# Attention in 128-query blocks of four heads, and a rearranged first chunk, in a fused sliding-window attention and MoE kernel on one core

## The chip, the cores and the metric

The kernel runs on one core of one Trainium2 chip. The core has a tensor engine (PE, with its weight loads shown apart as PEld), a vector engine (DVE), a scalar engine (ACT), GpSimd (POOL) and a queue engine (SP). POOL and SP issue the transfers between device memory and the on-chip buffers; sixteen DMA engines carry them out. The metric is the device time of one execution in microseconds (us). Lower is better.

## The reference

Attention over 8 batches, 8 heads, 576 tokens and head size 64, with a causal window of 128 tokens and a linear position bias per head; then, over the 4608 tokens of 512 features, a product with `w_in`, `h * cos(h)`, and a product with `w_out`. All inputs and the output are float32.

```python
B, H, S, D = q.shape                        # 8, 8, 576, 64
scores = 1.0 / np.sqrt(D) * np.matmul(q, k.transpose(0, 1, 3, 2))
rel = pos[:, None] - pos[None, :]
slopes = 2.0 ** (-8.0 * (np.arange(H) + 1) / H)
bias = slopes[:, None, None] * (-np.abs(rel))[None]
mask = (rel >= 0) & (rel < 128)
attn = softmax(np.where(mask, scores + bias[None], -1e9))
x = np.matmul(attn, v).transpose(0, 2, 1, 3).reshape(B * S, H * D)
h = x @ w_in                                # 512 x 2048
out = (h * np.cos(h)) @ w_out               # 2048 x 512
```

## The kernel before

All matrix work is in bf16, with float32 sums. The kernel is written as a list of operations, each with the buffers that it reads and writes, a cost and a priority. `Plan.schedule` plays this list once while the program is built: it gives each engine, at each step, the operation that can start soonest (within a slack, by priority) and so fixes the order of every engine. On the chip each engine runs its instructions in that order and waits on semaphores. Some operations (copies out of the matrix sums) may go to ACT or DVE; the planner picks. The planner's constants (`SWITCH`, the cost of changing between array modes; `TABLE`, of an ACT table load; `WIRE0`, when the first bytes move) decide only orders.

The tokens are cut into nine chunks of 512 (`CH`), which do not line up with the batches of 576.

- Loads. POOL issues q and k of batches 0 and 1 in a row-interleaved form (`qrows`, `krows`, cast to bf16 on the way), the v blocks, `w_in` in five pieces, `w_out` in four. For later batches it loads q and k as they lie (`qnat`, `knat`, one buffer each), and SP transposes them by DMA into `qt`, `kt` (lines 346 and 349). Batches 0 and 1 are transposed on PE against an identity (line 436) and copied out by ACT and DVE. `POOL` also makes the identity and the distance table `dif` (lines 373 to 384), after issuing its first two loads.
- Attention is done in units. A unit is one pair of heads over 256 queries (`G` 0 or 1), and one tail unit per batch takes all heads over the last 64 queries: nine units a batch. For a unit PE makes scores (line 488, two heads side by side in the two halves of the array's rows; the tail's on line 479), ACT takes the exponential (line 518), DVE multiplies by a table `emask` that holds mask and bias as factors (line 534), PE multiplies by v (lines 566 and 569; tail 553 and 555), and DVE divides by the sums (lines 604 and 606). The result goes, transposed, to `xT`: through PE and a copy (line 634, `x_pe`) if its chunk comes next, else by a DMA transpose on SP (`x_dma`). Units go in groups of two.
- MoE1 multiplies `xT` by `w_in` for one chunk in 16 column blocks of four products of 512 columns (line 670). ACT takes the cosine (as a sine with a shift), DVE multiplies into `gT` (two buffers). For chunk 0 this is done in halves of 256 tokens (line 693).
- MoE2 multiplies `gT` by `w_out`: four tiles of 128 tokens a chunk, 16 products of 512 columns each (line 716). ACT or DVE copies the tile to one of four output buffers `ob`, and SP stores it (line 728).

Before the first chunk nine units run, all of batch 0. Then, for chunk c, come MoE1 of c, a quota of units (`QUOTA`, 9, 9, 12, 12, 8, 8, 5) and MoE2 of c; the planner interleaves them. ACT needs one table for exponentials and another for the sine, so it changes tables twice a chunk. `load_v`, `dma_transposes` and `load_nat` for later batches are put in the list as units are done:

```python
while next_t < B and done >= 9 * (next_t - 1):
    dma_transposes(next_t)
    next_t += 1
    if next_t < B:
        load_nat("q", q, next_t)
        load_nat("k", k, next_t)
```

Of the kernel before, what the change touches and what calls it, by code (L numbers as in the profile page):

```python
# [13 lines left out]
NBLK = 5  # L14
# [20 lines left out]
class Plan:  # L35
# [3 lines left out]
    SWITCH = 95  # L39
    TABLE = 1330  # L40
    WIRE0 = 3700
# [46 lines left out]
    def schedule(self):  # L88
        free = {e: 0 for e in ENG}
        wire = {e: self.WIRE0 for e in ENG}  # L90
# [5 lines left out]
        def reach(o, e):  # L96
# [8 lines left out]
            return t  # L105
        for o in self.all:
            if o.npred == 0:
                avail.append(o)
        order = []
        while avail:  # L110
            phase = next((t for t in tables if left[t]), None)
            best = None
            for e in ENG:
                cand = []
                for o in avail:
                    if e not in o.eng or (o.table is not None and o.table != phase):
                        continue
                    st = max(free[e], reach(o, e))
                    if e == "pe" and o.mode != mode:
                        st += self.SWITCH  # L120
                    cand.append((st, o))
                if not cand:
                    continue
                soon = min(st for st, _ in cand)
                slack = 100 if e == "pe" else 40
                st, o = min(((st, o) for st, o in cand if st <= soon + slack),
                            key=lambda c: (c[1].pri, c[1].seq))
# [7 lines left out]
            if len(o.eng) > 1:  # L135
                o.fn, o.occ, o.lat = o.fn[e], o.occ[e], o.lat[e]
                o.eng = (e,)
            o.start = st
            free[e] = st + o.occ
            if o.dma is not None:  # L140
                wire[e] = max(wire[e], st + 2300) + o.lat
                o.end = max(wire[e], st + o.occ + 1400) + 500
# [12 lines left out]
        assert len(order) == len(self.all)  # L155
        self.span = max(o.end for o in order)
        self.order = sorted(order, key=lambda o: o.start)
        rank = {id(o): i for i, o in enumerate(order)}
        self.order.sort(key=lambda o: (o.start, rank[id(o)]))
# [81 lines left out]
def bass_alibi_sliding__then__act_gcu_kernel(  # L241
# [8 lines left out]
    with ExitStack() as ctx:  # L250
# [8 lines left out]
        XR = NTOK  # L259
        xT = sb("xT", [128, NPAIR, XR])  # L260
        gT = [sb(f"gT{i}", [128, NFC, CH]) for i in range(2)]
        qB = {"q": sb("qrows", [128, 2, 1152]), "k": sb("krows", [128, 2, 1152])}
# [3 lines left out]
        EM = sb("emask", [128, H, 512])  # L266
        EMt = sb("emtail", [128, H, 128])
        NP = 4
        P = [sb(f"p{i}", [128, 2, 512]) for i in range(NP)]
        Pt = [sb(f"ptail{i}", [128, 1088]) for i in range(2)]  # L270
        NX = 8
        xnat = [sb(f"xnat{i}", [128, 256]) for i in range(NX)]
        xtl = [sb(f"xtail{i}", [64, 512]) for i in range(2)]
        NCOS = 3
# [4 lines left out]
        ident = sb("ident", [128, 128])  # L279
        halfpi = sb("halfpi", [128, 1], F32)  # L280
# [4 lines left out]
        QUOTA = [9, 9, 12, 12, 8, 8, 5]  # L285
# [3 lines left out]


# [7 lines left out]
        def query_ap(b, x, pr, blk, width):  # L298
# [4 lines left out]
            t = t.rearrange("p (c k t) -> p c k t", c=NBLK, k=NPAIR)  # L303
            if width <= 128:
                return t[lo, blk, pr, 0:width]
            return t[lo, blk:blk + width // 128, pr, :]

        PIECES = {0: [(0, 8, [(0, 4), (4, 8)]), (256, 10, [(0, 5), (5, 10)])],  # L310
                  1: [(0, 18, [(0, 5), (5, 10), (10, 14), (14, 18)])]}

        def piece_keys(which, b, n):
            return [("qB", which, 0), ("qB", which, 1)] if b else [("qB", which, n)]

        def load_qk(which, src, b, n=0):
            t0, R, _ = PIECES[b][n]
            c0 = 64 * (t0 // 32)
            rows = bass.AP(src.tensor, src[b].offset + 64 * t0,
                           [[64 * R, 32], [64 * S, H], [1, 64 * R]])  # L320
            op("pool", [lambda e: e.dma_start(qB[which][:, :, c0:c0 + 64 * R], rows)],
               w=piece_keys(which, b, n), dma=f"ld{which}{n}", occ=800, lat=161 * R)
# [33 lines left out]
        def load_w_in(f0, f1):  # L356

# [3 lines left out]
               w=[("wi", f) for f in range(f0, f1)], dma=f"wi{f0}", occ=800,  # L361
               lat=1300 * (f1 - f0))

        def load_w_out(u):
# [3 lines left out]
               w=[("wo", u)], dma=f"wo{u}", occ=800, lat=2650)  # L368


        def constants():
            sel = ["sel"]
            op("pool", lambda e: e.memset(ident[:, :], 1.0), w=["ident"] + sel)
# [472 lines left out]
```

## Time and profile before

| what | value |
|---|---|
| median of 3 runs | 325.03 us |
| lowest and highest run | 322.65 and 328.85 us |
| span of the profiled execution, first to last instruction | 321.4 us |
| PE busy | 307.3 us |
| ACT, DVE, POOL busy | 203.9, 188.7, 96.6 us |
| read from and written to device memory | 36.70 and 9.44 MB |

The profile is of one execution; its own time is not given beside its span. A row of the timeline gives start, duration, engine, line, operation, output and inputs, and how many instructions; "L716" is line 716 of the kernel above. A matrix product's busy time includes its way through the array, so products that follow closely overlap, and the mean of one (379 ns for 512 columns) is longer than the distance between two. "Idle before" is the time for which an engine stood still, with what ended it.

### The profile page before, as it was taken

Reading aid. Unit: us, or ns where it says so; the run is one execution under the profiler, and the core shown is the slowest. Engines: PE = TensorE matmul, PEld = TensorE weight load, DVE = VectorE, ACT = ScalarE, POOL = GpSimd, SP = SyncE. Lnnn points to the kernel's source line nnn. Section 1 sums busy time; section 2 is a strip of 40 time slices with the busy share of each in tenths; the row PEclk is TensorE's granted clock in tenths of the full one; section 3 lists DMA queues with packets and bytes.
Section 4 is the critical chain, followed back from the end, with each engine's and each line's share of the span. In section 5 each row is a group of like instructions: output and inputs, shape, how many; then the busy total and the mean of one; then the engine's idle time right before and its main releaser. Section 6 shows DMA issues by size and latency. Waiting matters only on the chain.

```text
span 321.4 us, 6210 instructions
## 1 busy us (share of the span) xinstructions
PE 307.3 (96%) x2450; PEld 153.1 (48%) x2450; DVE 188.7 (59%) x414; ACT 203.9 (63%) x296; POOL 96.6 (30%) x124
## 2 busy tenths in 40 slices
PE   2789999999999999999999999999999999999995
PEld 2568745434544554455444544544444444444442
DVE  3689759674777677759684856564653550344000
ACT  5797865885688696866686676665674562453211
POOL 7997141355347572744507200000000000000000
PEclk9999999999999999999999999999999999999999
DMA  6999999999999999999999982131013001201121
GB/s 89 170 206 210 205 160 192 143 168 144 164 140 160 163 197 146 193 154 153 153 131 122 171 135 45 63 81 45 2 65 76 34 0 55 77 0 67 65 92 72
DMA packets 145004, 37.82 MB, mean 118 GB/s; under 512 B 134224, under 2 KB 139856, under 8 KB 144976
## 3 DMA queue, kind: packets, MB, share of 16 engines
q0 software_dynamic: 100144, 18.36, 74.7%
q1 hardware_dynamic: 44832, 19.08, 29.9%
q8 instruction: 19, 0.31, 0.4%
q14 instruction: 9, 0.07, 0.1%
HBM read 36.70 MB, written 9.44 MB: 144 GB/s over the span
## 4 chain that ended last, share of the span: by engine, by line
PE 82%; DMA 9%; POOL 4%; SPq 2%; issue 1%; ACT 1%; DVE 0%; POOLq 0%; ACTq 0%
PE ps L716 38%; PE ps L670 31%; DMA qrows<-in_q_dram 5%; PE ps L488 4%; DMA xT<-xnat 2%; PE ps L693 2%; DMA kt<-knat 2%; SPq L346 2%; PE ps L566 2%; PE ps L569 1%; POOL vp L327 1%; PE ps L634 1%; PE ps L436 1%; POOL w_inb L358 1%; PE ps L479 1%
## 5 line engine op out<-in xcount | busy, mean ns | idle before, releaser
L716 PE MATMUL ps<-w_outb,gT 128*128 128x512 bf16 x576 | 138.9, 379 | 0.0
L670 PE MATMUL ps<-xT,w_inb 128*128 128x512 bf16 x512 | 116.8, 379 | 0.8 <-DVE xnat L606 0.7
L679 DVE TENSOR_TENSOR gT<-ps,cos 128x512 bf16<-128x512 f32 x128 | 81.2, 685 | 51.0 <-PE ps L716 41.0
L675 ACT ACTIVATE cos<-ps,halfpi 128x512 f32<-128x512 f32 x128 | 81.3, 688 | 37.6 <-PE ps L716 19.1
L716 PEld LDWEIGHTS ps<-w_outb,gT 128*128 128x128 bf16 x576 | 53.6, 98 | 58.6 <-issue 1.9
L670 PEld LDWEIGHTS ps<-xT,w_inb 128*128 128x128 bf16 x512 | 47.2, 98 | 61.5 <-DVE gT L679 6.4
L518 ACT ACTIVATE p<-ps 128x768 bf16<-128x768 f32 (+1 forms) x64 | 55.8, 919 | 23.8 <-PE ps L488 18.7
L534 DVE TENSOR_TENSOR p<-p,emask 128x768 bf16<-128x768 bf16 (+1 forms) x64 | 38.3, 616 | 7.4 <-ACT p L518 6.8
L327 POOL DMA_DIRECT2D vp<-in_v_dram x40 | 33.8, 869 | 27.2 <-PE ps L569 16.2
L722 ACT ACTIVATE ob<-ps 128x512 f32<-128x512 f32 x24 | 14.4, 601 | 36.9 <-PE ps L716 36.8
L337 POOL DMA_DIRECT2D qnat<-in_q_dram x30 | 25.2, 875 | 28.4 <-DMA qt<-qnat 28.4
L337 POOL DMA_DIRECT2D knat<-in_k_dram x30 | 25.3, 875 | 25.7 <-DMA kt<-knat 23.7
L606 DVE TENSOR_TENSOR xnat<-ps,rec 128x256 bf16<-128x256 f32 x64 | 24.4, 420 | 1.1 <-DMA xT<-xnat 0.8
L488 PE MATMUL ps<-qt,kt 64*128 64x128 bf16 (+1 forms) x320 | 19.4, 247 | 1.4 <-DMA kt<-knat 1.2
L566 PEld LDWEIGHTS ps<-vp,p 128*128 128x128 bf16 x256 | 15.8, 98 | 7.1 <-issue 3.2
L566 PE MATMUL ps<-vp,p 128*128 128x65 bf16 x256 | 18.5, 195 | 0.0
L604 DVE RECIPROCAL rec<-ps 128x4 f32<-128x4 f32 x64 | 8.2, 167 | 17.4 <-PE ps L569 17.0
L488 PEld LDWEIGHTS ps<-qt,kt 64*128 64x128 bf16 x320 | 11.4, 96 | 13.2 <-issue 4.9
L569 PE MATMUL ps<-vp,p 128*128 128x65 bf16 x192 | 17.2, 194 | 0.0
L693 PE MATMUL ps<-xT,w_inb 128*128 128x256 bf16 x128 | 16.2, 273 | 0.8 <-ACT xT L643 0.5
L724 DVE COPY ob<-ps 128x512 f32<-128x512 f32 x12 | 8.3, 688 | 13.4 <-PE ps L716 13.4
L569 PEld LDWEIGHTS ps<-vp,p 128*128 128x128 bf16 x192 | 13.5, 98 | 0.5
(51 smaller groups left out, 167.6 us busy)
## 6 DMA issues: line engine op xcount, KB each, us to landing
out_dram<-ob SPq DMA_DIRECT2D x36, 256.0 KB, 2.1
vp<-in_v_dram POOLq DMA_DIRECT2D x32, 128.0 KB, 8.1
qnat<-in_q_dram POOLq DMA_DIRECT2D x24, 128.0 KB, 6.2
knat<-in_k_dram POOLq DMA_DIRECT2D x24, 128.0 KB, 4.9
w_outb<-in_moe_w_out_dram POOLq DMA_DIRECT2D x4, 512.0 KB, 21.8
w_inb<-in_moe_w_in_dram POOLq DMA_DIRECT2D x3, 512.0 KB, 10.6
qrows<-in_q_dram POOLq DMA_DIRECT2D x1, 576.0 KB, 14.9
krows<-in_k_dram POOLq DMA_DIRECT2D x1, 576.0 KB, 16.9
```

What stands on the lines that cost most here:

```text
L327: op("pool", [lambda e, t=t, rows=rows: e.dma_start(vp[b % 2][0:rows, t, :, 0:64], v[b, :, 128 * t:128 * t + rows, :].rearrange("h p d -> ...
L337: fns.append(lambda e, t=t, rows=rows: e.dma_start(nat[which][0:rows, t, :, :], src[b, :, 128 * t:128 * t + rows, :].rearrange("h p d -> p ...
L488: ins = e.matmul(ps[:, banks[x], c0:c1], keys_ap(b, x, pr, kc), query_ap(b, x, pr, qb, 128 * nb), start=True, stop=True)
L518: op("act", lambda e: e.activation(P[i][:, :, lo:512], src_[:, :, lo:512], ACTF.Exp, scale=0.125), w=held + [("P", i)], occ=920 if G else ...
L534: op("dve", lambda e: e.tensor_tensor(P[i][:, :, lo:512], P[i][:, :, lo:512], EM[:, h0:h1 + 1, lo:512], ALU.mult), r=[("P", i), ("EM", h0) ...
L566: ins = e.matmul(o, P[i][:, x, d0:d0 + 128], V[:, kc, h, 0:65], start=True, stop=not two)
L569: ins = e.matmul(o, P[i][:, x, p0:p0 + 128], V[:, kc - 1, h, 0:65], start=False, stop=True)
L606: op("dve", lambda e: e.tensor_tensor(o, U[:, :, :, 0:64], rv[:, :, :, None].broadcast_to([128, 2, 2, 64]), ALU.mult), r=[("rec", n % 2)], ...
L670: op("pe", lambda e, kc=kc: e.matmul(ps[:, bank, :], w_in[:, kc, 128 * fc:128 * fc + 128], xT[:, kc, r0:r0 + CH], start=(kc == 0), stop=(k ...
L675: op("act", lambda e: e.activation(cosb[ci][:, :], ps[:, bank, :], ACTF.Sin, bias=halfpi[:, 0:1]), r=["halfpi"], w=[("B", bank), ("cos", c ...
L679: op("dve", lambda e: e.tensor_tensor(gT[gi][:, fc, :], ps[:, bank, :], cosb[ci][:, :], ALU.mult), r=[("cos", ci)], w=[("B", bank), ("g", ...
L716: op("pe", lambda e, t=t, fc=fc, bank=bank: e.matmul(ps[:, bank, :], gT[gi][:, fc, 128 * t:128 * t + 128], w_out[:, fc, :], start=(fc == 0 ...
```

## The change

- A unit is now one block of 128 queries by four heads (`(b, qb, hh)`, `qb` 1 to 3). The first block of a batch, whose window holds no earlier keys, is one unit of all eight heads, and so is the 64-query tail: eight units a batch. Scores are always 128 columns wide (64 in the tail). All eight-head units use both sum banks `UB`; a batch's first block is normalised into a new buffer `xfirst` and transposed in four.
- Seven units, the 512 tokens of chunk 0, come before the first chunk; quotas are 8, 8, 8, 8, 8, 8, 9, and the later loads follow `8 * (next - 1)`.
- MoE1 of chunk 0 goes by blocks of 128 tokens and four column blocks.
- q and k of batch 0 come in three pieces instead of two. The first (128 tokens) is loaded by SP in float32 and cast by ACT or DVE (`qcast`, `kcast`). POOL makes its constants before its loads, and the loads are interleaved in a new order.
- For three of the first units the bias is added by PE, as a product of the identity with a table `bias`, before the scores are summed on top; these units skip the multiplication on DVE. `emask` is made from `bias` by two exponentials.
- PE starts with 19 products of a block of zeros.
- The very last output tile is made and stored as 384 and 128 columns.
- The planner has start times for each engine, doubled PE costs before 8 us, other costs for loads, and another rule of choice for PE.

In the built program PE has 448 + 128 score products instead of 320 + 128, 576 products with v as before, 48 + 32 + 28 transposes of x instead of 66, 128 transposes in the row-interleaved form and 8 whole ones instead of 144, and 256 products for MoE1 of chunk 0 instead of 128. SP transposes 25 results by DMA instead of 39.

```diff
-    SWITCH = 95
+    SWITCH = 110
     TABLE = 1330
-    WIRE0 = 3700
+    START = {"pe": 1300, "act": 750, "dve": 1050, "pool": 550, "sp": 750}
+    COLD = 8000
+    FILL = 107
...
+        def pick_pe(cand):
+            soon = min(st for st, _ in cand)
+            first = [(st, o) for st, o in cand if o.pri < 5 and st <= soon + 160]
+            if first:
+                return min(first, key=lambda c: (c[1].pri, c[1].seq))
+            near = [(st, o) for st, o in cand if st <= soon]
+            return min(near, key=lambda c: (c[1].pri, c[1].seq))
...
-        QUOTA = [9, 9, 12, 12, 8, 8, 5]
+        QUOTA = [8, 8, 8, 8, 8, 8, 9]
+        BIASED = [(0, 0, 0), (0, 1, 0), (0, 1, 1)]
...
-        PIECES = {0: [(0, 8, [(0, 4), (4, 8)]), (256, 10, [(0, 5), (5, 10)])],
+        PIECES = {0: [(0, 4, [(0, 4)]), (128, 4, [(0, 4)]), (256, 10, [(0, 5), (5, 10)])],
...
+            if b == 0 and n == 0:
+                op("sp", [lambda e: e.dma_start(qF[which][:, :, :], rows)],
+                   w=[("qF", which)], dma=f"ld{which}f", occ=400, lat=600)
+                i = qF[which][:, :, :].rearrange("p y (j d) -> p y j d", j=4)
+                o = qC[which][:, :, :, :].rearrange("p j y d -> p y j d")
+                op(("act", "dve"),
+                   {"act": lambda e: e.activation(o, i, ACTF.Copy),
+                    "dve": lambda e: e.tensor_copy(o, i)},
+                   r=[("qF", which)], w=piece_keys(which, b, n), occ={"act": 460, "dve": 330},
...
         def masks():
+            flat = dif[:, :, :].rearrange("p a b -> p (a b)")
             for h in range(H):
...
+                    "dve": lambda e, o=o, s=s: e.tensor_scalar(o, flat, s, None, ALU.mult)},
+                   r=["dif"], w=[("BT", h)], occ={"act": 310, "dve": 250},
+                   lat={"act": 410, "dve": 330}, pri=3)
+            for x in range(2):
+                op("act", lambda e, x=x: e.activation(
+                    EM[:, x, :, :], BT[:, x, :, :], ACTF.Exp, scale=0.125),
...
         def units(b):
-            return [(b, pr, G) for G in range(2) for pr in range(NPAIR)] + [(b, "t", None)]
+            return [(b, 0, 0)] + [(b, qb, hh) for qb in range(1, 4) for hh in range(2)] + [
+                (b, 4, 0)]
...
+                    if qb == 0:
+                        jobs = [(128 * pr, 128, pr, 0) for pr in range(NPAIR)]
+                    elif qb == 4:
+                        jobs = [(128 * pr + 64 * i, 64, pr, 3 + i) for pr in range(NPAIR)
+                                for i in range(2)]
+                    else:
+                        jobs = [(256 * i + 128 * j, 128, 2 * hh + i, qb - 1 + j)
+                                for i in range(2) for j in range(2)]
...
+                        op("pe", lambda e, rhs=rhs, bank=bank: e.matmul(
+                            ps[:, bank, :], ident[:, :], rhs, start=True, stop=False),
...
+        def moe1_block(t, f4, bank):
+            for i in range(4):
+                    for kc in range(NPAIR):
+                        ins = e.matmul(
+                            ps[:, bank, 128 * i:128 * i + 128],
+                            w_in[:, kc, 128 * fc:128 * fc + 128], xT[:, kc, t0:t0 + 128],
...
+                for n, (j0, j1) in enumerate([(0, 384), (384, 512)] if last else [(0, 512)]):
...
         load_qk("q", q, 0, 1)
         load_qk("k", k, 0, 1)
-        load_v(0)
+        load_v(0, [0])
+        load_qk("q", q, 0, 2)
+        load_qk("k", k, 0, 2)
+        load_v(0, [1])
+        load_w_in(0, 1)
+        load_v(0, [2])
+        load_w_in(1, 2)
+        load_v(0, [3])
+        load_w_in(2, 4)
+        load_w_in(4, 6)
...
         load_qk("q", q, 1)
+        load_w_in(6, 8)
         load_qk("k", k, 1)
+        load_v(0, [4])
...
-        attention(every[0:9], -1)
-        done = 9
+        done = 7
+        attention(every[0:done], -1)
...
+                order = [(0, 0), (1, 0), (2, 0), (0, 1), (1, 1), (2, 1), (3, 0), (3, 1)] + [
+                    (t, f4) for f4 in (2, 3) for t in range(4)]
+                for i, (t, f4) in enumerate(order):
+                    moe1_block(t, f4, seq[i % 6])
...
-        R.schedule()
+        R.schedule(filler=lambda e: e.matmul(ps[:, UB[1], 0:128], zeros[:, :], zeros[:, :],
+                                             start=True, stop=True), fill=(1300, 7500))
```

496 lines of the change are left out of this document (259 added, 237 removed).

## The prediction

> **What bounds the kernel now.** I read the page first, then busy time by stage, then the chain of waits in the stretches where the stages show idle time, then the loads.
>
> ```profile
> span 321.4 us, 6210 instructions
> ...
> PE 307.3 (96%) x2450; PEld 153.1 (48%) x2450; DVE 188.7 (59%) x414; ACT 203.9 (63%) x296; POOL 96.6 (30%) x124
> ```
>
> ```profile
> 0.00:20.80 20.80, 12.07 (x182) 8.21 (x183) 12.96 (x38) 14.43 (x24) 19.09 (x32) 1.00 1.26 147
> 20.80:38.90 18.10, 17.95 (x241) 14.96 (x238) 15.20 (x31) 15.01 (x24) 11.27 (x14) 1.00 1.20 207
> 38.90:72.90 34.00, 32.82 (x269) 15.65 (x268) 24.45 (x54) 24.41 (x35) 11.68 (x14) 1.00 1.95 167
> 72.90:289.20 216.30, 215.53 (x1636) 101.34 (x1637) 132.40 (x286) 142.91 (x203) 54.55 (x65) 1.00 1.00 106
> ```
>
> The second fence is busy time by stage: the stretch, its length, then busy time of PE, weight loads, DVE, ACT, POOL, then granted clock, DMA share, GB/s. From 20.8 us on PE hardly rests; before that 8.7 us are idle, and a good part of the 12.1 "busy" is slow or small. So nothing but the front, a few waits and PE's own work can move the time. The front ends where MoE2 of chunk 0 starts, at 38.9. I split the span there: 38.9 of front, 282.5 behind it.
>
> What sets the 38.9? The chain of waits from 14 to 40 us, and the issues and landings of the loads (line, KB each, us to landing; the last row is the w_in tile's minimum, median, maximum):
>
> ```profile
> 14.24 14.86 DMA qrows<-in_q_dram
> ...
> 32.07 0.68 PE ps L436 x20
> ...
> 34.17 0.62 PE ps L436 x16
> ...
> 36.42 0.57 PE ps L436 x16
> 36.99 2.07 PE ps L693 x18
> 39.06 1.08 PE ps L716 x5
> ```
>
> ```profile
> 1.32 0.83 POOL L321 DMA_DIRECT2D qrows<-in_q_dram  x1 [0.81 <-POOLq L831]
> 2.15 0.72 POOL L321 DMA_DIRECT2D krows<-in_k_dram  x1
> 2.86 0.22 POOL L373 MEMSET ident<- 128x128 bf16 x1
> 4.45 0.29 POOL L384 TENSOR_SCALAR_AFFINE_SELECT dif<-dif 128x128 f32<-128x128 f32 x1
> 4.89 0.75 POOL L321 DMA_DIRECT2D qrows<-in_q_dram  x1 [0.15 <-issue]
> 5.64 0.71 POOL L321 DMA_DIRECT2D krows<-in_k_dram  x1
> 10.57 3.75 POOL L358 DMA_DIRECT2D w_inb<-in_moe_w_in_dram  x5
> 14.94 0.71 POOL L321 DMA_DIRECT2D krows<-in_k_dram  x1
> ```
>
> ```profile
> krows<-in_k_dram POOLq DMA_DIRECT2D x1, 576.0 KB, 16.9
> qrows<-in_q_dram POOLq DMA_DIRECT2D x1, 320.0 KB, 4.4
> krows<-in_k_dram POOLq DMA_DIRECT2D x1, 320.0 KB, 6.0
> krows<-in_k_dram POOLq DMA_DIRECT2D x1, 256.0 KB, 4.8
> ```
>
> ```profile
> DMA to landing us min/median/max: 6.2/8.8/12.4
> ```
>
> POOL issues its loads long before they land: they stand in one queue and land in order. Batch 1's k was issued at 14.94 and landed at 14.94 + 16.9 = 31.8; its transposes run at 32.07, and what hangs behind them fills PE until 38.9, 7.1 us later. The rate: w_in's first piece lands at 10.57 + 6.2 = 16.8, the last (issued about 13.5) at 25.9, so 1792 KB in 9.1 us, 197 KB/us. So the front is a stream of loads up to batch 1's k, plus 7.1 us.
>
> **The front after the change.** Four things move that landing.
> - POOL makes its constants before its first load. They take 2.86 to 4.74, 1.9 us; the first load goes from 1.3 to about 3.0: +1.7 (bounds 1.4 and 1.9).
> - The same constants no longer cut the stream. Batch 0's first k landed at 2.15 + 4.8 = 6.9, the second q only at 4.89 + 4.4 = 9.3 and the second k at 5.64 + 6.0 = 11.6; 320 KB should take 1.6 each by the rate, and took 2.4 and 2.3: -1.5.
> - The first 128 tokens of q and k (128 KB each as bf16) come over SP's queue in float32: -256/197 = -1.3.
> - The fifth block of v (64 KB) goes behind batch 1's k: -0.3.
>
> SP's two float32 loads (issued under 1.5 us) use the DMA engines while the POOL stream has not begun, which hides them; without that cover they hold twice the bytes, at most 512/197 = 2.6 us. Sum -1.4: k lands at 30.4 (29.5 to 32).
>
> Behind that landing stand, in the built order, the same 20 + 16 + 16 transposes of 64 columns (0.68 + 0.57 + 0.57), and 60 MoE1 products of 128 columns where 44 of 256 stood. Before, 18 took 2.07 with one switch of array mode, so 0.109 each; half is 0.055. The trace's nearest whole 128-wide products are x transposes, two in 0.16. I take 0.058 (0.055 to 0.08): 3.5, with switches 5.6. Front: 30.4 + 5.6 = **36.0**, 2.9 less.
>
> Is PE ready for that? The stream's first 256 KB should land at 3.0 + 4.8 = 7.8, and the first w_in piece 1152 KB later, at 13.7 instead of 16.8. From there PE has 256 x 0.058 = 14.8 of MoE1, 2.5 of batch 1's four transposes with 0.6 of switches, and about 4 of attention (four units at 0.3 of scores, 0.3 of p-v, 0.2 of x, and switches): 35.6. ACT was busy 15.0 of 18.1 us in that stage and has two exponentials fewer. So the stream is last, by 0.4 us; the earlier start of attention, the bias on PE (six 512-wide products while PE waits), the zero products and the earlier casts all end in a wait for the stream, and I price them at nothing. If the stream were earlier, PE would be next, so 0.4 us is all they can add.
>
> **Behind the front.** Rows from the chain of waits, the kt tile's transposes (ns minimum/median/maximum) and the waits table (longest in the last column):
>
> ```profile
> 58.52 7.08 SPq L346
> ...
> 65.64 7.20 DMA kt<-knat
> ...
> 72.88 0.50 PE ps L488 x8
> 73.39 3.13 PE ps L716 x14
> 76.52 0.44 PE ps L488 x8
> 76.95 0.32 PE ps L716
> ...
> 78.50 0.16 PE ps L634 x2
> 78.66 0.22 PE ps L716
> 78.99 0.55 PE ps L488 x12
> ```
>
> ```profile
> L346 SPq DMA_TRANSPOSE kt<-knat x6: 2672/3455/7078, 58.5 to 183.8; - x6
> ```
>
> ```profile
> PE ps L488 <- DMA kt<-knat: 1.2, 1, 1.2
> PE ps L670 <- DVE xnat L606: 0.7, 1, 0.7
> ```
>
> - Score groups: columns and p-v products are the same in sum, but the built order has 29 groups behind the front instead of 33. A lone MoE2 product after a group takes 0.32 instead of 0.22, and the way in costs as much: 4 x 0.22 = -0.9. 16 products of 128 keep the 0.55 of 12.
> - Seven units, not nine, precede the front; their sums leave batch 0's tail behind it: 16 p-v products and a quarter of a group, +0.7.
> - x through PE: behind the front 25 pairs become 18 pairs, 7 transposes of four (a batch's first block) and 7 narrow ones of four: 25 x 0.16 = 4.0 becomes 2.9 + 2.2 + 1.3 = 6.4: +2.4. SP loses 14 of 39 x transposes.
> - Wait for batch 2's kt, 1.2. PE reaches those scores with 73 MoE2 products done where it had 57, so at 36.0 + 137 x 0.216 + 6.4 = 72.0 (before, 72.9 - 1.2 - 38.9 less 121 x 0.216 left 6.7 for one unit more). kt: its transposes follow the same stream, 1.4 earlier, so 71.5 or before; v of batch 3 is no longer queued ahead of them. -1.2 (0 to -1.2).
> - Wait for x at 156, 0.7: x by DMA is now needed a whole chunk later. -0.7.
> - Uniform quotas of 8, six P buffers, the planner's new constants: no price of their own, 0 ± 1; PE is 99.6% busy in that stage.
>
> ```profile
> 318.20 0.60 ACT ob L722
> ...
> out_dram<-ob SPq DMA_DIRECT2D x36, 256.0 KB, 2.1
> ```
>
> - The last tile is split 384/128: the last copy shrinks from 0.60 to about 0.27, the last product ends 0.16 sooner, the store of 64 KB may save 0.2; the 384 part is stored while PE still works. -0.7.
>
> Sum -0.9 + 0.7 + 2.4 - 1.2 - 0.7 - 0.7 = -0.4: 282.1 behind the front. Span 36.0 + 282.1 = **318.1**, 3.3 under this profile's. The profile's 321.4 lies 1.25 under the fastest time, 322.65, and 3.6 under the median of 325.03; of launch and end nothing is shown, so I carry the difference to the median: **321.7 us**.
>
> **A rule against it.** POOL's issues are 0.69 to 0.95 long wherever DVE stands:
>
> ```profile
> L327 POOL DMA_DIRECT2D vp<-in_v_dram x20: 687/877/945, 6.4 to 59.2; - x20
> ```
>
> The Trainium skill, SBUF — State Buffer, section "Who interferes with whom", says that a VectorE operation in a two-port mode, float32 copies among them, locks GpSimd out of writing descriptors. The change puts two such casts and four bias products on DVE just when POOL writes its first descriptors. By that rule the stream would slip by their length, by the planner's own costs 4 x 0.25 + 2 x 0.33 = 1.7 us, an estimate; the row's spread of 0.26 bounds it far lower. As a mechanism of this kernel it is rival B.
>
> **Rivals.**
> - A: the runs that make the median lie up to 6 us over the fastest (322.65 to 328.85), and what can lengthen a run here is a late transfer: kt at 72.9 is waited for already, and up to 12 units a chunk were demanded. At 8 units a batch is due every 33 us, so after could lose that too, 3.6: 325.0 - 3.3 - 3.6 = 318.1. Against: the one wait shown is 1.2, no more. 0.36.
> - B: the stream is not earlier, since constants first, float32 loads and DVE's port work take back the 1.4 and more: front 38.5, 325 or a little under. 0.10.
> - C, slower: SP's queue. Batch 3's transposes stand ahead of MoE2 stores, and each pair held SP's queue from 58.5 to landing for 14 us. If qt must also wait for the loads of q, which now wait for the transposes before them, stores stop, four output buffers fill, and PE stands. It decides once a chunk's 28 us of transposes plus stores and x exceed 33; one chunk in each batch at 2 us gives 12: 333. Against: the median issue of kt is half of this first one's, and 14 x transposes leave SP. 0.09.
>
> My forecast has 0.45. Two per cent, about what a measurement of this kernel can tell from no change, is 6.5 us. Faster by more: two thirds of A and a fifth of the forecast, 0.33; slower: C, 0.09; within: 0.58. Range: the forecast's own terms give 319 to 325; with A and B 315 to 326.5.
>
> **What would show it.** MoE2 of chunk 0 starts at 36 (38 or later: B), batch 1's k lands near 30.4, the scores of batch 2 begin near 72 with no wait on kt, no x wait over 0.3 later, end behind the last product 2.6 instead of 3.2. PE standing behind full output banks between 70 and 250 us would be C. If the front is 36 and the span not under 320, my price for x through PE is wrong.

## The result and the profile after

The kernel after took 321.6 us (median of 12 runs, 320.88 to 322.64) beside 322.86 for the kernel before on the same chip: ratio 0.9956, 95% interval 0.9937 to 0.9976. Run once more later, beside other versions, it took 320.73 against 324.16: 0.9902, 0.9867 to 0.9936. So there is a gain, between 0.2 and 1.3%; the two ratios differ mostly by the kernel before, whose median was 322.86 in one set and 324.16 in the other. The time agrees with the 321.7 that was forecast, but its parts don't: the front did not shrink, what lies behind it shrank by more than forecast, and the step from span to time was half of the one carried over. That the sum agrees is luck. One version below, x by DMA, was profiled in an execution of 334.28, over 1.5% longer than its fastest of 328.65, so its figures by stage are of a slow execution.

The page of the kernel after, then its busy time by stage (columns as in the prediction: stretch, length, PE, weight loads, DVE, ACT, POOL, granted clock, DMA share, GB/s):

```profile
span 320.0 us, 6788 instructions
...
PE 307.2 (96%) x2741; PEld 163.0 (51%) x2781; DVE 196.9 (62%) x424; ACT 203.4 (64%) x277; POOL 96.6 (30%) x124
```

```profile
0.00:8.00 8.00, 5.88 (x55) 3.64 (x55) 5.50 (x23) 4.95 (x8) 6.71 (x16) 1.00 0.78 120
8.00:16.00 8.00, 3.72 (x55) 2.73 (x58) 2.21 (x5) 3.31 (x6) 5.84 (x8) 0.79 1.49 167
16.00:24.00 8.00, 7.53 (x148) 5.87 (x145) 6.42 (x18) 7.35 (x9) 6.92 (x10) 1.00 1.36 204
24.00:39.50 15.50, 15.29 (x297) 14.37 (x296) 13.15 (x23) 12.48 (x20) 10.98 (x14) 1.00 1.24 206
39.50:320.00 280.50, 274.74 (x2197) 136.37 (x2234) 169.60 (x356) 175.26 (x238) 66.19 (x79) 1.00 1.02 107
```

PE is nearly full from 16 us on; the hole is in the second row, where it is busy for 3.7 us of 8. The chain of waits of the front (start, length, what) shows whose hole it is, and the PE timeline what was waited for:

```profile
5.37 7.33 DMA qrows<-in_q_dram
...
17.60 0.38 PE ps L756 x4
...
39.50 1.67 PE ps L784 x7
```

```profile
12.74 1.28 PE L483 MATMUL ps<-ident,qrows 128*64 128x128 bf16 x20 [3.12 <-DMA qrows<-in_q_dram]
14.35 0.63 PE L555 MATMUL ps<-bias,ident 128*128 128x512 bf16 x1 [0.33 <-issue]
14.78 0.63 PE L675 MATMUL ps<-ident,xfirst 128*128 128x128 bf16 x4
15.35 0.56 PE L541 MATMUL ps<-qt,kt 64*128 64x128 bf16 x8
15.83 0.75 PE L483 MATMUL ps<-ident,krows 128*64 128x128 bf16 x20
...
33.66 0.75 PE L483 MATMUL ps<-ident,krows 128*64 128x128 bf16 x20
```

The third piece of q (320 KB; "the large piece" below) was issued at 5.37 and landed 7.33 us later; PE stood for 3.12 us in front of its transposes, while bias products, x transposes and scores that needed nothing from it stood behind them in PE's fixed order. MoE1 began at 17.60, MoE2 of chunk 0, "MoE2(0)" below, at 39.50. So the front is 39.5 (before 38.9), and 280.5 lie behind it (before 282.5). The load that the prediction took for the last of the stream, batch 1's k, was issued at 17.13 and landed at 32.73 (31.83 in the kernel before, 30.4 in the forecast). PE came to its transposes at 33.66, the last row, 0.9 later: in this profile PE was last, and not the stream.

Behind the front the waits table has nothing left over 0.2 us, and the last copy starts 2.4 us ahead of the end, where it was 3.2:

```profile
PE ps L784 <- issue: 1.6, 10, 0.2
```

```profile
316.71 0.49 ACT L791 ACTIVATE ob<-ps 128x384 f32<-128x384 f32 x1 [2.00 <-PE ps L784]
...
317.60 0.28 ACT L791 ACTIVATE ob<-ps 128x128 f32<-128x128 f32 x1 [0.40 <-PE ps L784]
```

### The profile page after: what moved, and what is told of

It is laid out like the page before. It is cut to its first block, busy times and chain, and to the rows that moved or that the text cites. A ratio compares the mean times of both kernels' runs of the same rounds, so it can differ in the third digit from the quotient of the medians.

```text
span 320.0 us, 6788 instructions
## 1 busy us (share of the span) xinstructions
PE 307.2 (96%) x2741; PEld 163.0 (51%) x2781; DVE 196.9 (62%) x424; ACT 203.4 (64%) x277; POOL 96.6 (30%) x124
## 4 chain that ended last, share of the span: by engine, by line
PE 90%; ACT 3%; DMA 2%; issue 2%; POOL 1%; DVE 1%; ACTq 0%; POOLq 0%
PE ps L784 39%; PE ps L731 32%; PE ps L541 5%; PE ps L756 4%; DMA qrows<-in_q_dram 2%; PE ps L615 2%; PE ps L617 2%; ACT p L568 2%; PE ps L483 1%; PE ps L675 1%; PE ps L603 1%; PE ps L694 1%; DVE gT L740 1%; ACT cos L736 1%; PE ps L607 1%
## 5 line engine op out<-in xcount | busy, mean ns | idle before, releaser
L784 PE MATMUL ps<-w_outb,gT 128*128 128x512 bf16 (+2 forms) x566 | 133.2, 373 | 2.4 <-issue 1.6
L731 PE MATMUL ps<-xT,w_inb 128*128 128x512 bf16 x499 | 113.2, 379 | 0.7
L568 ACT ACTIVATE p<-ps 128x1024 bf16<-128x1024 f32 x64 | 62.0, 1021 | 30.4 <-PE ps L541 30.3
L731 PEld LDWEIGHTS ps<-xT,w_inb 128*128 128x128 bf16 x512 | 48.9, 98 | 59.1 <-DVE gT L740 3.5
L587 DVE TENSOR_TENSOR p<-p,emask 128x1024 bf16<-128x1024 bf16 x61 | 41.0, 684 | 6.4 <-ACT p L568 6.2
L791 ACT ACTIVATE ob<-ps 128x512 f32<-128x512 f32 (+2 forms) x25 | 14.5, 581 | 36.8 <-PE ps L784 36.8
L654 DVE TENSOR_TENSOR xnat<-ps,rec 128x256 bf16<-128x256 f32 x48 | 18.3, 419 | 0.1
L756 PE MATMUL ps<-xT,w_inb 128*128 128x128 bf16 x256 | 16.8, 219 | 0.2 <-DVE rec L652 0.2
L615 PEld LDWEIGHTS ps<-vp,p 128*128 128x128 bf16 x192 | 12.7, 97 | 7.2 <-issue 6.4
L615 PE MATMUL ps<-vp,p 128*128 128x65 bf16 x192 | 15.2, 193 | 0.3
L617 PE MATMUL ps<-vp,p 128*128 128x65 bf16 x192 | 15.2, 193 | 0.0
L756 PEld LDWEIGHTS ps<-xT,w_inb 128*128 128x128 bf16 x256 | 14.5, 98 | 0.9 <-issue 0.3
L617 PEld LDWEIGHTS ps<-vp,p 128*128 128x128 bf16 x192 | 12.5, 97 | 0.0
## 6 DMA issues: line engine op xcount, KB each, us to landing
w_outb<-in_moe_w_out_dram POOLq DMA_DIRECT2D x4, 512.0 KB, 19.8
```

What stands on the lines that cost most here:

```text
L568: op("act", lambda e: e.activation(P[i][:, 0:1024], ps[:, banks[0]:banks[0] + 2, :].rearrange("p a b -> p (a b)"), ACTF.Exp, scale=0.125), ...
L587: op("dve", lambda e: e.tensor_tensor(p, p, m, ALU.mult), r=[("P", i), ("EM", 0), ("EM", 1)], w=[("P", i)], occ=600, lat=690, pri=1)
L615: e.matmul(o, P[i][:, c0:c0 + 128], V[:, qb - 1, h, 0:65], start=True, stop=False)
L617: ins = e.matmul(o, P[i][:, c0 + 128:c0 + 256], V[:, qb, h, 0:65], start=False, stop=True)
L731: op("pe", lambda e, kc=kc: e.matmul(ps[:, bank, :], w_in[:, kc, 128 * fc:128 * fc + 128], xT[:, kc, r0:r0 + CH], start=(kc == 0), stop=(k ...
L756: ins = e.matmul(ps[:, bank, 128 * i:128 * i + 128], w_in[:, kc, 128 * fc:128 * fc + 128], xT[:, kc, t0:t0 + 128], start=(kc == 0), stop=( ...
```

## The experiments

The question was what holds the front at 39.5: the stream of loads (theory S), PE's own added work and its order (P), or DVE holding back POOL's descriptors (D, the prediction's rival B). All versions start from the kernel after. The table collects them; medians and ratios are against the kernel before in the same set, the other columns come from each version's one profile. "k" is batch 1's k: when it landed, and when PE came to its transposes.

| version | median us | ratio (95% interval) | large piece of q landed | k landed, reached | MoE2(0) starts | behind it |
|---|---|---|---|---|---|---|
| after | 321.6 | 0.9956 (0.9937 to 0.9976) | 12.70 | 32.73, 33.66 | 39.50 | 280.5 |
| after, again | 320.73 | 0.9902 (0.9867 to 0.9936) | 11.53 | 32.78, 32.82 | 38.43 | 280.7 |
| last tile whole | 321.9 | 0.9939 (0.9913 to 0.9965) | 11.35 | 31.39, 32.51 | 38.13 | 281.5 |
| v early | 320.75 | 0.9913 (0.9885 to 0.9941) | 12.67 | 33.06, 34.26 | 39.88 | 280.3 |
| no zero products | 321.21 | 0.9924 (0.9898 to 0.9950) | 11.89 | 31.93, 33.47 | 39.31 | 280.5 |
| POOL loads before constants | 320.71 | 0.9909 (0.9882 to 0.9935) | 10.92 | 32.82, 32.87 | 38.58 | 280.5 |
| first q, k by POOL in bf16 | 324.66 | 1.0022 (0.9993 to 1.0052) | 13.08 | 33.12, 34.23 | 40.30 | 280.9 |
| wait filled | 321.85 | 0.9948 (0.9924 to 0.9971) | 11.39 | 32.06, 33.44 | 39.06 | 281.1 |
| x by DMA | 332.39 | 1.0234 (1.018 to 1.0288) | 11.41 | 33.01, 33.06 | 38.55 | 294.0 |
| MoE1 in halves | 320.67 | 0.9914 (0.988 to 0.9948) | 12.23 | 32.22, 33.20 | 37.68 | 281.9 |
| no bias on PE | 323.0 | 0.9977 (0.9947 to 1.0006) | 12.69 | 32.69, 35.35 | 41.20 | 281.1 |
| loads first, v later | 320.41 | 0.9882 (0.985 to 0.9914) | 9.55 | 31.71, 31.75 | 37.59 | 281.1 |
| the same, in halves | 319.78 | 0.9864 (0.9832 to 0.9896) | 9.73 | 31.47, 31.51 | 37.48 | 280.6 |

The k column shows a second limit of the front, which was not among the theories. In five profiles PE comes to the transposes of batch 1's k 0.04 or 0.05 us behind its landing, and in three of them the row shows a wait, as here:

```profile
32.87 0.75 PE L483 MATMUL ps<-ident,krows 128*64 128x128 bf16 x20 [1.03 <-DMA krows<-in_k_dram]
```

```profile
31.75 0.75 PE L483 MATMUL ps<-ident,krows 128*64 128x128 bf16 x20 [0.40 <-DMA krows<-in_k_dram]
```

The first row is of the version with POOL's loads before its constants, the second of the one with v later; with x by DMA the wait is 0.39. From PE's start on these transposes MoE2(0) follows 5.5 to 6.1 us later in all versions but halves (4.5). So the stream up to batch 1's k plus some 5.6, the prediction's own limit, holds the front where PE would come to these transposes earlier.

**The same kernel again.**

> The kernel after, once more, beside the three others of this set. In four profiles with its early order on PE the large piece of q landed at 11.35 to 12.70, by how far one of the 16 DMA engines lagged, and MoE2(0) started 26.8 to 27.4 us behind that landing. Theory S: so again here, front = landing + 27.0 within 0.5, and 280.5 behind it. Theory P (PE alone sets the front): MoE2(0) at 39.5 wherever the piece lands.

From PE's timeline of this second profile:

```profile
11.57 1.28 PE L483 MATMUL ps<-ident,qrows 128*64 128x128 bf16 x20 [0.74 <-DMA qrows<-in_q_dram]
...
38.43 1.89 PE L784 MATMUL ps<-w_outb,gT 128*128 128x512 bf16 x8
```

The piece landed 1.17 sooner, and MoE2(0) started 1.07 sooner. Over the four profiles that share PE's order (after twice, last tile whole, v early) the front is the landing plus 26.8 to 27.2. S holds here; P, which had 39.5 whatever lands, falls. The first w_in piece moves along with it (front 23.0 to 23.3 behind its landing), but what PE's first MoE1 product waits for last is DVE (0.16 to 0.47 in these four), with w_in there 1.1 us or more before.

**Without the zero products.**

```diff
-    start=True, stop=True), fill=(1300, 7500))
+    start=True, stop=True), fill=(0, 0))
```

> The kernel after without its 19 zero products; nothing else moves. Theory S (stream): the front, up to MoE2 of chunk 0, is set by when the second large piece of q (320 KB) and the first w_in piece land (12.7 and 16.5 us), with about 22 us of PE work behind w_in. The zero products end in that wait, so MoE2(0) still starts at 39.5 and the time moves by less than 0.3 us. Theory P (PE): PE's own early work sets the front, so its first products run at a lower clock without the zeros, the granted clock falls in the slices after 4 us, and the front grows by 0.5 to 1 us.

```profile
11.93 1.28 PE L483 MATMUL ps<-ident,qrows 128*64 128x128 bf16 x20 [1.32 <-DMA qrows<-in_q_dram]
...
39.31 1.67 PE L784 MATMUL ps<-w_outb,gT 128*128 128x512 bf16 x7
```

PE's early products were slower (see the last section), and the front is landing plus 27.4, 0.2 to 0.6 more than with the zeros; the runs (320.19 to 323.52) can't be told from the kernel after's. About 0.6 us at most, then.

**POOL's first two loads ahead of its constants.**

```diff
-        constants()
         load_qk("q", q, 0, 1)
         load_qk("k", k, 0, 1)
+        constants()
```

> POOL issues its two loads of q and k (tokens 128 to 255) before it makes its constants, as the kernel before did with its first loads. If the stream's volume from POOL's first issue on sets the landing of the second large piece of q (12.7), that piece lands 1 to 1.6 us sooner and MoE2(0) starts at 38 to 38.5. If that landing follows from its own issue (5.37, unmoved here, since POOL does the same work before it), it stays near 12.7 and the front at 39.5; the first landings alone (6.1 and 7.1) come 1.6 sooner.

```profile
10.96 0.75 PE L483 MATMUL ps<-ident,qrows 128*64 128x128 bf16 x20 [1.17 <-DMA qrows<-in_q_dram]
...
38.58 1.67 PE L784 MATMUL ps<-w_outb,gT 128*128 128x512 bf16 x7
```

The piece was issued 0.6 later than in the kernel after (5.98) and landed 1.8 sooner (10.92; 0.6 sooner than in the second profile): neither reading as written. MoE2(0) gained less than the piece, since PE then stood 1.03 for batch 1's k; without that wait the front would be some 37.6, an estimate from these rows. What differs is in the landings of the piece's 16 parts, one for each DMA engine. From its issue to the median of the 16 it takes 4.24 to 4.77 us in thirteen of the fourteen kernels (5.03 in one), the kernel before included; from the median to the last it takes:

```
before 0.17, POOL loads first 0.56, loads first and v later 0.41, the same in halves 0.41
after 2.75, again 1.39, last tile whole 1.24, v early 2.56, no zeros 1.73, no bias 2.45,
wait filled 1.12, halves 2.05, x by DMA 1.00, first q and k by POOL 1.15
```

In the first row nothing or one load is issued directly ahead of the piece (the constants come between); in the others three loads follow each other without a pause, and the last part comes 1.0 to 2.75 us behind the median, in most profiles with one to three others 0.7 or more behind it too. So the landing of this piece is its own issue plus about 4.5, plus a laggard. The smaller loads ahead of it took less, 2.9 to 4.3 to the median of theirs.

**The first 128 tokens over POOL's queue in bf16.** SP's float32 loads and DVE's casts are gone.

```diff
-            if b == 0 and n == 0:
+            if False:
...
-            whole = b == 0 and n == 0
+            whole = False
```

> The first 128 tokens of q and k come over POOL's queue in bf16, as in the kernel before, instead of over SP's in float32 with casts on DVE. POOL gets two more issues, about 1.6 us, ahead of all else. Theory S: the large piece of q and all behind it land 1.3 to 1.6 us later and MoE2(0) starts near 41. Theory D (the float32 loads or the two DVE casts hold the stream back, as a rule on DVE and POOL sharing a port would have it): without them the piece lands no later than 12.7 for all that, POOL's issues of 0.70 to 0.92 become shorter, and the front stays or shrinks.

```profile
13.12 0.75 PE L483 MATMUL ps<-ident,qrows 128*64 128x128 bf16 x20 [0.30 <-DMA qrows<-in_q_dram]
...
40.30 1.67 PE L784 MATMUL ps<-w_outb,gT 128*128 128x512 bf16 x7
```

The piece was issued 1.9 later (7.28), its median engine had it 2.0 later, and the ratio rose to 1.0022 from 0.9902 to 0.9956, 2 to 4 us. Without the casts the piece took the usual 4.65 from its issue to the median, so D is not what made it late. The two casts and the issues beside them, first in the kernel after, then in the version with MoE1 in halves:

```profile
4.19 0.53 DVE L360 CAST qcast<-qfirst 128x512 bf16<-128x512 f32 x1 [0.45 <-DMA qfirst<-in_q_dram]
4.82 0.81 DVE L360 CAST kcast<-kfirst 128x512 bf16<-128x512 f32 x1
3.78 0.72 POOL L364 DMA_DIRECT2D krows<-in_k_dram  x1
4.49 0.89 POOL L370 DMA_DIRECT2D vp<-in_v_dram  x1
5.37 0.70 POOL L364 DMA_DIRECT2D qrows<-in_q_dram  x1
```

```profile
4.00 0.43 DVE L360 CAST qcast<-qfirst 128x512 bf16<-128x512 f32 x1 [0.26 <-DMA qfirst<-in_q_dram]
4.68 0.43 DVE L360 CAST kcast<-kfirst 128x512 bf16<-128x512 f32 x1 [0.25 <-DMA kfirst<-in_k_dram]
3.78 0.79 POOL L364 DMA_DIRECT2D krows<-in_k_dram  x1
4.57 1.02 POOL L370 DMA_DIRECT2D vp<-in_v_dram  x1
5.58 0.70 POOL L364 DMA_DIRECT2D qrows<-in_q_dram  x1
```

Of a cast and the issue beside it, one is stretched. In the nine profiles with this order of POOL's issues, k's issue takes 0.72 where the first cast takes 0.53 to 0.62, and 0.78 to 0.83 where that cast takes 0.43; v's takes 0.89 where the second cast takes 0.60 to 0.87, and 1.02 to 1.06 where that one takes 0.43. The rule of the Trainium skill, SBUF — State Buffer, section "Who interferes with whom", by which these casts can shut POOL out of writing descriptors, agrees with these rows. But it is small here: the large piece is issued at 5.37 to 5.67 in these nine, so 0.3 us at most, where rival B needed 1.4 and more.

**The wait filled.** The planner is told that the large piece lands 2.5 us later.

```diff
-               ..., lat=161 * rr)
+               ..., lat=161 * rr + (2500 if b == 0 and n == 2 and which == "q" else 0))
```

> The planner is told that the large piece of q lands 2.5 us later than it believed, so PE's order has two bias products, eight scores and the four transposes of the first block ahead of that piece's transposes instead of behind them. Theory S with a fixed order: 1.5 to 1.8 us of PE work moves into the wait of 3.1 us (9.6 to 12.7), and as PE has no gap behind it, MoE2(0) starts 1 to 1.8 us sooner, at 37.7 to 38.5. Theory W (w_in's landing at 16.5 alone decides): MoE1 still starts near 17 and the front shrinks by 0.5 at most. The order behind the front changes too, so that part may move by 0.5 either way.

```profile
11.95 1.27 PE L484 MATMUL ps<-ident,qrows 128*64 128x128 bf16 x20
14.28 1.28 PE L484 MATMUL ps<-ident,krows 128*64 128x128 bf16 x20 [1.06 <-ACT qt L498]
...
39.06 1.89 PE L785 MATMUL ps<-w_outb,gT 128*128 128x512 bf16 x8
```

A miss. The work did move into the wait, but PE then waited 1.06 for a copy, ran its products at the slow pace until 18 us, and the front is landing plus 27.7. Shifting this work bought nothing. That the chain from q over scores, exponentials, p-v and x to MoE1 is last fits this, but this version doesn't separate it from the slow pace.

**MoE1 of chunk 0 in halves of 256 tokens.**

```diff
+        def moe1_half(hf, f2, bank):
...
-                order = [(0, 0), (1, 0), (2, 0), (0, 1), ...]
-                    moe1_block(t, f4, seq[i % 6])
+                order = [(0, f2) for f2 in range(8)] + [(1, f2) for f2 in range(8)]
+                    moe1_half(hf, f2, seq[i % 6])
```

> MoE1 of chunk 0 goes in halves of 256 tokens and two column blocks, as in the kernel before, instead of blocks of 128 tokens and four; all else is of the kernel after, with the order that the planner makes of it. Theory S (the front is the landing of the early loads and then PE's work): 128 products of 256 cost 14.0 where 256 of 128 cost 14.8, but the first can start only when all of x for 256 tokens is there, some 1 us later, so MoE2(0) starts between 38.5 and 40 and the part behind stays at 280.5. Rival (the blocks of 128 are what keeps PE fed before 20 us): the idle time of PE between 16 and 24 us grows from 0.5 to over 2 and the front exceeds 41.

```profile
37.68 1.46 PE L813 MATMUL ps<-w_outb,gT 128*128 128x512 bf16 x6
```

Neither reading: MoE2(0) starts sooner than both have it and 281.9 lie behind it, since the planner leaves some of batch 1's transposes for later; the sum, 319.6 with the piece at 12.23, is what the kernel after has at such a landing. Blocks of 128 buy nothing, halves cost nothing.

**No bias on PE.**

```diff
-        BIASED = [(0, 0, 0), (0, 1, 0), (0, 1, 1)]
+        BIASED = []
```

> No unit gets its bias from PE: the six products of 512 columns are gone, the first three units are multiplied by the mask table on DVE like the others, and the planner makes another early order from that. The prediction priced the bias on PE at nothing, since it ends in the wait for the loads. Theory S: the front stays at the landing of the large piece of q + 27 within 0.7, the time within 0.3% of the kernel after's. Rival (three masks fewer on DVE are what the early units gain by): masks of about 0.9 us each stand between exponentials and p-v products of the first units, first x is later by 1 to 2, and the front exceeds landing + 28.

From PE's timeline, and one row of DVE's:

```profile
12.73 1.28 PE L483 MATMUL ps<-ident,qrows 128*64 128x128 bf16 x20 [2.79 <-DMA qrows<-in_q_dram]
15.65 1.28 PE L483 MATMUL ps<-ident,krows 128*64 128x128 bf16 x20 [1.08 <-DVE qt L498]
...
41.20 1.89 PE L784 MATMUL ps<-w_outb,gT 128*128 128x512 bf16 x8
```

```profile
14.60 0.21 DVE L640 RECIPROCAL rec<-ps 128x8 f32<-128x8 f32 x1 [3.67 <-PE ps L603]
```

The piece landed when it did in the kernel after (12.69, 12.70), and MoE2(0) started 1.7 later; the median is 2.3 above the kernel after's in the same set (323.0, 320.73). The rival came out: the front is landing plus 28.5. In the kernel after the first p-v products run at 9.22, ahead of the wait; here the mask of 0.7 us stands before them, they come behind the large piece's transposes, and the first reciprocal is at 14.60 instead of 9.66. Part of the 1.7 is PE's pace, which stayed low until 20 us in this profile; how much is the masks' and how much the pace's was not separated.

**Loads first and the first v block later; then also in halves.** The first version has the edit of "POOL's first two loads ahead of its constants" and this one:

```diff
-        load_v(0, [0])
         load_qk("q", q, 0, 2)
         load_qk("k", k, 0, 2)
+        load_v(0, [0])
         load_v(0, [1])
```

> POOL's first two loads ahead of its constants, as in the version of that name, and the first block of v behind the large pieces of q and k instead of ahead of them. In that earlier version the large piece of q was issued at 5.98 and landed at 10.9. Theory S1 (that piece lands some 4.5 us behind its own issue): it is issued at 4.9 to 5.1, lands at 9.5 to 10, and as PE's early work hangs on it, MoE2(0) starts at 37.5 to 38, against 38.6; span 318 to 318.7. Theory S2 (by then w_in's landing near 15.5 and 22 us of PE behind it set the front): it stays at 38 to 38.6.

> The version before this, with MoE1 of chunk 0 in halves of 256 tokens as well. If blocks of 128 buy nothing once the loads are there (span with halves 319.6 where the large piece of q landed at 12.2), the span is within 0.5 of the version with blocks; if they let PE start MoE1 sooner, it is 0.5 to 1.5 longer.

```profile
9.86 0.75 PE L483 MATMUL ps<-ident,qrows 128*64 128x128 bf16 x20 [0.16 <-DVE kt L498]
...
37.59 1.89 PE L784 MATMUL ps<-w_outb,gT 128*128 128x512 bf16 x8
```

S1's numbers came: landed at 9.55, front 37.6, span 318.7; with halves as well 318.1, 0.6 shorter, which neither reading had. This last version beats both kernels: 319.78, 0.9864 of before, and its six runs lie within 319.67 to 319.95, below every run of the kernel after (320.39 to 322.89 in the same set). The front is now 28 behind the landing: the piece is no longer alone in setting it. Part of this is the 0.40 for which PE stands in front of batch 1's k (landed at 31.71, the row shown under the table). To shorten the front further that load would have to come sooner too.

**Behind the front: x by DMA, v early, the last tile whole.**

```diff
-    after.append((t_first(u) // CH > phase + 1, u, ub, n))
+    after.append((t_first(u) // CH > phase + 1 or (phase > 0 and u[1] in (0, 4)), u, ub, n))
```

> The kernel after, but behind the first chunk the results of a batch's first block and of its tail go to xT by SP's DMA transpose (12 more on SP) instead of through PE and a copy. Theory X (the price of the prediction holds: 0.32 for four transposes of 128, 0.19 for four narrow ones): the part behind the start of MoE2 of chunk 0, 280.5 in every version of the kernel after so far, shrinks by 6 x 0.32 + 6 x 0.19 = 3.1 to 277.4, the front stays, and the time falls by 1%. Theory Y (they cost more, some 0.44 a group with the way in and out): by up to 5. Theory Z (they were cheap or the DMA comes too late): waits on xT or on SP's queue, of xfirst's reuse above all, take their place, and that part stays within 1 of 280.5 or grows.

Z, and worse: 294.0 in the profiled execution, and some 288 by the fastest run (an estimate: 328.65 less 1.8 from span to time and the front of 38.55). From the rows of SP, then of PE:

```profile
82.23 5.15 SPq L389 DMA_TRANSPOSE kt<-knat  x1
87.42 2.05 SPq L392 DMA_TRANSPOSE kt<-knat  x1
...
92.04 1.26 SPq L714 DMA_TRANSPOSE xT<-xfirst  x1
```

```profile
100.07 15.83 PE L731 MATMUL ps<-xT,w_inb 128*128 128x512 bf16 x64 [7.77 <-DMA xT<-xfirst]
...
136.10 13.97 PE L731 MATMUL ps<-xT,w_inb 128*128 128x512 bf16 x64 [0.52 <-issue]
```

The x transpose stands in SP's queue behind kt's transposes and stores and lands 8 us after its issue, and MoE1 of a whole chunk waits for it. In this execution the wait costs twice: behind it the 64 products take 15.83, in the next chunk 13.97. x through PE, at its price, keeps this wait away.

Next, v one unit earlier:

```diff
-            while next_v < B and done >= 8 * (next_v - 1):
+            while next_v < B and done >= 8 * (next_v - 1) - 1:
```

> The v blocks of the batch after next are put in POOL's queue one unit earlier, as in the kernel before, so that they stand ahead of the loads of q and k of the next batch and wait there for the buffer of the batch before. Orders of PE, DVE, ACT and SP are the same. If that is what made kt late in the kernel before: kt of batch 2, landed at 68.3 in the kernel after, lands later only if POOL's next loads hold it, which they don't for this first one, but that of batch 3 does; a wait on kt or qt of 0.5 us or more returns somewhere behind 100 us and the part behind the front grows from 280.5 by that. If the earlier stream and the later units alone removed the wait: no wait, 280.5.

(In this version the tail unit of a batch multiplies by the v of two batches later; the amount of work is the same.) No wait came back: 280.3. But kt did become late. From this version's POOL, then from its kt tile, and the same last row of the kernel after:

```profile
53.84 0.88 POOL L370 DMA_DIRECT2D vp<-in_v_dram  x1 [5.71 <-PE ps L617]
...
58.86 2.44 POOL L370 DMA_DIRECT2D vp<-in_v_dram  x3 [1.79 <-PE ps L617]
```

```profile
DMA to landing us min/median/max: 2.4/5.4/13.2
```

```profile
DMA to landing us min/median/max: 3.7/7.3/8.7
```

The v loads are issued just ahead of and beside the first kt transposes, which are issued 1.2 later and land at 73.8 instead of 68.3. PE comes to the scores only at 76.0 (75.4 in the kernel after, 71.7 before), so nothing waits. By these times either an earlier kt or a later PE would have removed the wait of 1.2; my expectation, a wait behind 100 us or no late kt, was wrong.

Last, the output tile in one piece:

```diff
-                for n, (j0, j1) in enumerate([(0, 384), (384, 512)] if last else [(0, 512)]):
+                for n, (j0, j1) in enumerate([(0, 512)]):
```

> The last output tile in one piece of 512 columns, with one copy and one store, as in the kernel before; the order of everything else is the same. By the prediction the split is worth 0.7: the part behind the front grows from 280.5 to 281.2, and the end lies 3.2 to 3.7 behind the start of the last product where it lay 2.7 behind. If the split is worth nothing (the store's own latency sets the end): 280.5.

```profile
316.38 0.60 ACT L791 ACTIVATE ob<-ps 128x512 f32<-128x512 f32 x1 [2.86 <-PE ps L784]
```

281.5 lie behind the front instead of 280.5, and the end is 3.2 behind this copy's start (span 319.6) where it is 2.4 behind the last copy's in the kernel after. The split is worth 1.0 in the span behind the front; the medians, whose fronts differ by up to 1.4, can't show it.

## Why the prediction came out right, and where it did not

The forecast of 321.7 had a front 2.9 shorter, 0.4 less behind it, and 3.6 from span to median. The profiles have a front 0.6 longer (0.5 shorter in the second profile), 1.8 to 2.0 less behind it, and 1.7 to 1.9 from span to time in every run. The errors cancel, so the number is right by luck; the two limits of the front that the prediction named, the stream and PE, are the ones that the runs show.

- **The landing of the stream: wrong, by 2.3 to 2.8.** Batch 1's k was to land at 30.4 and landed at 32.73 and 32.78 (32 was the upper bound); the first w_in piece was to land at 13.7 and landed at 16.46. The first 256 KB were there at 7.06 (forecast 7.8), and the 704 KB behind the large piece of q took 3.76, as the rate of 197 KB/us gives (3.57). All 3904 KB from behind that piece up to batch 1's k took 20.0 (19.8 by the rate). Nearly the whole miss lies between: v's first block and the large piece, 448 KB, took 5.64 instead of 2.3. That rate was read from w_in's loads, which stood in a full queue; the large piece's median part lands 4.2 to 5.0 us behind its own issue in all fourteen kernels. So the step "same constants no longer cut the stream: -1.5" failed: in the kernel before, too, the piece took 4.2, with the constants directly ahead of it, and behind three loads without a pause the last part lagged. This lag stayed in the stream: of batch 1's k the median part landed at 30.75 (30.90 before), the last one 2.0 later (0.9 before).
- **The work behind the stream: right.** 5.6 us were counted from batch 1's k to MoE2(0); from its transposes at 33.66 and 32.82 it took 5.8 and 5.6. 21.9 us were counted from the first w_in piece to MoE2(0); from MoE1's start at 17.60 it took 21.9. The stream was to be last by 0.4: PE was last by 0.9 in the first profile, and they met in the second. What the sum left out is the chain from the large piece of q to the first x: with w_in there at 14.34 (loads first, v later) MoE1 still began at 16.68.
- **Priced at nothing.** Zero products: 0.6 at most. Bias on PE: wrong, without it, in the order that the planner then makes, the front is 1.7 longer and the time 2.3. "All end in a wait for the stream" overlooked that with the bias the first p-v products come before the wait, and without it behind it.
- **Rival B** came out by its sign for the front (38 or later) and in that the stream is not earlier, but not by its mechanism or its time of 325: casts hold POOL back by 0.3 at most, and taking them and the float32 loads out, at the price of two more issues by POOL, costs 2 to 4 us. The constants ahead of the loads, priced at 1.7, can't be told from nothing in the time (0.9909 without, 0.9902 to 0.9956 with).
- **Behind the front: better by 1.4 than forecast.** PE's time is worked out here from the starts of consecutive products, in the second profile against the kernel before: waits for kt and x 1.9 less (forecast 1.9; kt of batch 2 landed at 69.6, and at 68.3 in the first profile, forecast 71.5 or before); x through PE 5.3 instead of 3.3, +2.0 (+2.4); scores and p-v products +1.9 and the gaps around MoE products -2.8, so -0.9 in sum (forecast -0.9 + 0.7 = -0.2); the tail -1.0 (-0.7). The signs were right. The price of x was 0.4 too high, that of the tail 0.3 too low; why the gaps around MoE products shrank by 2.8, for four score groups fewer, was not looked into. The scores of batch 2 began 35.9 behind the front's end, as forecast (36.0).
- **Rival C** did not come. The version with x by DMA shows a neighbour of it: 12 transposes more on SP's queue make 332 us, but through an x that lands late, not through full output buffers.
- **Rival A** stays open. Of the kernel before's 69 runs in the later sets 39 are above 323.6, the others near 322.9; of the kernel after's 20 runs five are above 322. The 3.6 carried to the median was 1.8 of fixed time, and for the rest this. What makes the difference is not known.

## What to carry to other kernels

A rate read from a full queue says little of the first loads: here they landed 3 to 5 us behind their own issue, so order them by who is waited for first, and don't count a hole in the issues as lost unless a landing behind it moves. When one wait is shortened, look which wait PE meets next: here it was batch 1's k, 20 us later. In an order that is fixed when the program is built, ask of each long wait what ready work stands behind it, and whether it is the chain or the work that is last, before pricing an edit ahead of it at nothing. And before moving work to a queue that is idle on average, look at what stands in it when the result is due.

## What the runs showed of the hardware

- The last of the large piece's 16 parts landed 1.0 to 2.75 us behind the median when three loads were issued directly ahead of it, in ten profiles of ten, and 0.2 to 0.6 in the four others. The two versions with the least lag of those made from the kernel after (0.41) also have the narrowest runs, 320.23 to 320.49 and 319.67 to 319.95. The cause is not known.
- Where a float32 cast on DVE and a load issue on POOL overlapped, one of the two was longer, in nine profiles of nine: the cast of 128x512 took 0.53 to 0.87 instead of 0.43, or k's issue 0.78 to 0.83 instead of 0.72 and v's 1.02 to 1.06 instead of 0.89.
- The same 20 transposes took 1.28 in some profiles and 0.75 in others. Without zero products all early ones were slow until 17 us though the granted-clock row stands at 1.00 there; with them they were fast from 5.7 to 9.5 in the kernel after and slow again behind the wait of 3.12. The Trainium skill, TensorE: Matmul & The Clock Gate, section "HAM oscillation — how this bites in real kernels", says that a wait for data between products can send the clock back to half; the kernel after agrees, and in its second profile the products were slow from 8.4 us on, right behind a wait of only 1.06. Early in a program the products' own durations tell the pace, not the clock row.
